# Decode attention with Mish: wq of the first pair whole ahead of the keys, b1 in one transfer, the residual in seven small transfers

## The chip, the core and the metric

The kernel runs on one core of one Trainium2 chip. TensorE (PE) multiplies, VectorE (DVE), ScalarE (ACT) and GpSimd (POOL) do the elementwise work, and SyncE (SP) issues most transfers between the chip's HBM and the on-chip memory SBUF. The transfers of all issuers are carried by the core's 16 DMA engines. The metric is the time of one execution on the device in microseconds. Everything is float32.

## The reference

Eight decode tokens, each with its own cache of 8192 keys and values for 8 key/value heads; four query heads share one of these. Beside the attention runs a dense block with Mish, and both are added to the input.

```python
xn = _layernorm(x, axis=-1)                                     # x: 8 x 1 x 512
q = (xn @ wq).reshape(B, 1, 32, 128)                            # wq: 512 x 4096
scores = einsum("bhqd,bhkd->bhqk", q, k) * (128 ** -0.5)        # k, v: 8 x 8 x 8192 x 128
o = einsum("bhqk,bhkd->bhqd", _softmax(scores), v)
A = o.reshape(B, 1, 4096) @ wo
h = xn @ w1 + b1                                                # w1: 512 x 1792
act = h * tanh(softplus(h))
return x + A + act @ w2
```

## The kernel before

**Units.** The key/value heads are taken in four pairs, and a unit is one pair of heads of one token: 32 units, numbered j, eight tokens b for each pair m. A unit's keys are 128 partitions of 64 KB (8.39 MB), its values are as large. The main loop (L483) runs over the units and does, for unit j: the scores in two halves (L316), a softmax (L328 to L349), the values of unit j - 1 (L378), the key weights of unit j + 1 (L299), the turning of the probabilities into the form that the value product needs (L355 to L366), and the merge of unit j - 1 (L395). The program's order is written out by hand; nothing is rescheduled. Each engine runs its own instructions in that order and waits only for what it needs.

**Places in SBUF.** One large tile `kv` holds what streams in. Values of all units, and the keys of unit 0, go to V_AT = 0. Keys of later units go alternately to two places (`K_AT`) that overlap by half: 16384 (even units) and 24576 (odd units), each 16384 elements wide. At 16384 also lie, at the start, the rows of x and the LayerNorm's scratch, then w1 (7168 elements) with b1 behind it, and then Mish's scratch. A second tile, `ws`, holds wq's columns of one pair (2 MB when whole).

**The loads on SP's queue.** SP issues, in order: three quarters of wq for pair 0 (L153), the keys of unit 0 (K0, through `load_unit`, L131), w1 (L476), the keys of unit 1 (K1), the values of unit 0 (V0), K2, V1, K3 and so on; wq for the later pairs (L125) comes in between, and wo and w2 at the end. An issue waits on SP until its place is free: V0 waits for the scores of unit 0, which read K0 at the same place; K2 waits until Mish has done with its scratch and until the first half of unit 1's scores has been read; V1 waits for the value product of unit 0.

**The last quarter of wq.** For pair 0 the projection `project(0)` (L245) takes its last 128 rows of wq from another place: `q0_x`, 32 partitions of `kv` at column 24576 (`XAT`), the place of the odd units' keys. Four transfers from POOL's queue (L150) fill it, alternating with four for b1 (L147), each of 8 partitions. Those issues stand on POOL ahead of the identity matrix (L158), the constants and the memsets, from which VectorE makes its selection matrices before it starts the LayerNorm (L188 to L201). Because three quarters of wq lie on 128 partitions and one quarter on 32, the transposed input exists in two extra forms, `xn3` (L208, L220) and `xnx` (L212, L221), beside `xn4`, which the later pairs use, and `xnT`, which Mish uses. A half of `project(0)` is three products on `ws` and four on `q0_x` (L255), then a copy by ACT (L263) and four small products (L266). `spread` (L281, L288) and `key_weights` (L299) follow before the scores of unit 0 can start.

**The residual.** x, as the last addition (L550) wants it, 8 rows at each of partitions 0, 32, 64 and 96, is made at the start by four products from `x_sb` with a copy into `xres` (L224 to L232).

Of the kernel before, what the change touches and what calls it, by code (L numbers as in the profile page):

```python
# [8 lines left out]
F32 = mybir.dt.float32  # L9
# [4 lines left out]
P = 128  # L14
B = 8
# [9 lines left out]
G = 4  # L25
NH = 2
TG = SK // (NH * G) // P
BW = 1024
CC = D // P
FG = F // G  # L30
FT = 4
FP = FG // FT
Q = P // G
# [4 lines left out]
ROW = NB * P * BW // P  # L38
# [13 lines left out]

D3 = 3
XQ = slice(64, 96)
XAT = ROW + ROW // 2

V_AT = 0
K_AT = (ROW, ROW + ROW // 2)
W1_AT = ROW
# [2 lines left out]


LOAD_Q, MAKE_Q, SPREAD_Q = 4, 5, 7


@with_exitstack
def kernel(
# [12 lines left out]
    nc = tc.nc  # L85
    PSUM = bass.MemoryType.PSUM

    const = ctx.enter_context(tc.tile_pool(name="const", bufs=1))
# [4 lines left out]
    kv = const.tile([P, PLACES], F32, name="kv")  # L93
    ws = const.tile([P, CC * BW], F32, name="ws")
# [4 lines left out]
    M = psum.tile([P, 512], F32, name="m")  # L99
    H = psum.tile([P, 512], F32, name="h")  # L100

    ident = const.tile([P, P], F32, name="ident")
# [7 lines left out]
    gsel = const.tile([B, B, B], F32, name="gsel")  # L110
    xn4 = const.tile([P, CC, B], F32, name="xn4")
    xnT = const.tile([P, CC, B], F32, name="xnT")
    xn3 = const.tile([P, D3, B], F32, name="xn3")
    xnx = const.tile([P, CC, B], F32, name="xnx")
    qr = const.tile([P, DI, H2 * B], F32, name="qr")
    xres = const.tile([P, P], F32, name="xres")
    oT = const.tile([P, NP, H2, B], F32, name="oT")
# [4 lines left out]
    def load_q(m):  # L122

        rows = wq.rearrange("j p f -> (j p f)").rearrange("(m p f) -> m p f", m=NP, p=P)
        nc.sync.dma_start(ws, rows[m])  # L125

    def load_unit(src, j, at):
        m, b = divmod(j, B)
        lo = (b * HKV + 2 * m) * NH * G
        t = kv[:, at : at + ROW]  # L130
        nc.sync.dma_start(  # L131
            t,
            src[lo : lo + NB].rearrange("j p f -> (j p f)").rearrange("(p f) -> p f", p=P),
        )
        return t
# [3 lines left out]
    x_sb, xc, sq = (low[:, i * D : (i + 1) * D] for i in range(3))  # L139
    nc.scalar.dma_start(x_sb, x)  # L140
    b1_sb = kv[:B, W1_AT + 7168 : W1_AT + 7168 + FG // 2]
    q0 = wq[:CC].rearrange("j p f -> (j p) f")
    q0_3 = ws[:, : D3 * BW]
    q0_x = kv[XQ, XAT : XAT + CC * BW]
    for r in range(4):
        n = FG // 8
        nc.gpsimd.dma_start(  # L147
            b1_sb[:, n * r : n * (r + 1)], b1.rearrange("(g c f) -> c g f", g=B, c=4)[r]
        )
        nc.gpsimd.dma_start(  # L150
            q0_x[r::4], q0[D3 * P :].rearrange("(e r i) f -> r e (i f)", r=4, i=CC)[r]
        )
    nc.sync.dma_start(q0_3, q0[: D3 * P].rearrange("(p i) f -> p (i f)", i=D3))  # L153
    k_t = {0: load_unit(kT, 0, V_AT)}
    w1_t = kv[:, W1_AT : W1_AT + 7168].rearrange("p (j f) -> p j f", j=2 * CC)

# [47 lines left out]
    for c in range(CC):  # L204
        nc.tensor.transpose(
            M[:, 32 + c * B : 32 + (c + 1) * B], xc[:, c * P : (c + 1) * P], ident[:B, :B]
        )
    for c in range(D3):  # L208
        nc.tensor.transpose(
            M[:, 64 + c * B : 64 + (c + 1) * B], xc[:, c : D3 * P : D3], ident[:B, :B]  # L210
        )
    for c in range(CC):  # L212
        nc.tensor.matmul(
            M[XQ, 96 + c * B : 96 + (c + 1) * B],
            xc[:, D3 * P + c :: CC],
            ident[:B, :B],
            start=True,
            stop=True,
        )
    nc.vector.tensor_copy(xn3.rearrange("p c b -> p (c b)"), M[:, 64 : 64 + D3 * B])  # L220
    nc.vector.tensor_copy(xnx[XQ].rearrange("p c b -> p (c b)"), M[XQ, 96:128])  # L221
    nc.vector.tensor_copy(xn4.rearrange("p c b -> p (c b)"), M[:, 0:32])
    nc.vector.tensor_copy(xnT.rearrange("p c b -> p (c b)"), M[:, 32:64])
    for g in range(G):  # L224
        nc.tensor.matmul(
            M[Q * g : Q * g + B, 256:384],
            ident[:B, :B],
            x_sb[:, g * P : (g + 1) * P],
            start=True,
            stop=True,  # L230
        )
    nc.vector.tensor_copy(xres, M[:, 256:384])  # L232
    wide = tr.rearrange("p y c -> p (y c)").rearrange("p (i o) -> p i o", i=DI)

    def selections():
# [9 lines left out]
    def project(m):  # L245

        w = ws.rearrange("p (c f) -> p c f", c=CC)
        terms = [(c, xn4[:, c, :], w[:, c]) for c in range(CC)]
        if m == 0:
            wx = q0_x.rearrange("p (c f) -> p c f", c=CC)  # L250
            terms = [(c, xn3[:, c, :], w[:, c]) for c in range(D3)]
            terms += [((c + D3) % CC, xnx[XQ, c, :], wx[:, c]) for c in range(CC)]
        for d in range(2):
            for n, (c, xt, wt) in enumerate(terms):
                nc.tensor.matmul(  # L255
                    H[Q * c : Q * c + B, :],
                    xt,
                    wt[:, d * 512 : (d + 1) * 512],
                    start=(n < CC),
                    stop=(n >= len(terms) - CC),  # L260
                )
            qp = work.tile([P, 512], F32, name="e")
            nc.scalar.copy(qp, H)  # L263
            for h in range(REP):
                at = 192 + (d * REP + h) * B
                nc.tensor.matmul(  # L266
                    M[:, at : at + B],
                    qp[:, h * DH : (h + 1) * DH],
                    bsel[:, :B],
                    start=True,  # L270
                    stop=True,
                )
        qT = work.tile([P, H2 * B], F32, name="qT", bufs=1)
        nc.vector.tensor_scalar_mul(qT, M[:, 192 : 192 + H2 * B], DH**-0.5)
        return qT
# [18 lines left out]
    def key_weights(j):  # L294
        b = j % B
        w = WK[j] = work.tile([P, DI, 2, NH * G, REP], F32, name="wk", bufs=1)
        q = qr.rearrange("p i (d o h b) -> p i d o h b", d=2, o=1, b=B)[..., b]
        for d in range(2):
            nc.vector.tensor_mul(  # L299
                w[:, :, d],  # L300
                q[:, :, d].to_broadcast([P, DI, NH * G, REP]),
                mask[:, d * NH * G : (d + 1) * NH * G]
                .rearrange("p (o k r) -> p o k r", o=1, r=1)
                .to_broadcast([P, DI, NH * G, REP]),
            )


    def scores(j, k, first, part):

        w = WK[j]  # L310
        lo = 0 if first else DI // 2
        kk = k.rearrange("p (i c f) -> p i c f", i=DI, c=HALF)
        for n in range(DI // 2):
            i = lo + n
            for c in range(HALF):
                nc.tensor.matmul(  # L316
                    S[64 * c : 64 * (c + 1), :],
                    w[:, i].rearrange("p d k h -> p (d k h)"),
                    kk[:, i, c, :],
                    start=(part == 0 and n == 0),  # L320
                    stop=(part == 1 and n == DI // 2 - 1),
                )
# [51 lines left out]
    def values(j, vt):  # L374
        for n in range(NJ):
            l, c = divmod(n, HALF)
            q = n % G
            nc.tensor.matmul(  # L378
                O[Q * q : Q * (q + 1), :],
                pt8[:, c, TL * l : TL * (l + 1), :].rearrange("p t h -> p (t h)"),  # L380
                vt[:, 512 * n : 512 * (n + 1)],
                start=(n < G),
                stop=(n >= NJ - G),
            )
        os = work.tile([P, DH], F32, name="os", bufs=1)
        nc.vector.tensor_scalar(os, O[:, :DH], isel[:, 0:1], None, op0=ALU.mult)  # L386
        for i in range(1, TL):
            nc.vector.scalar_tensor_tensor(  # L388
                os, O[:, DH * i : DH * (i + 1)], isel[:, i : i + 1], os, op0=ALU.mult, op1=ALU.add
            )  # L390
        return os
# [87 lines left out]
    spread(qT)  # L479
    key_weights(0)  # L480

    v_t = {}
    for j in range(UNITS):  # L483
        b = j % B
        more = j // B + 1 < NP

        k = k_t.pop(j)
        scores(j, k, j % 2 == 1, 0)
        if j == UNITS - 1:
            v_t[j] = load_unit(v, j, K_AT[0])  # L490
        elif j > 0:
            k_t[j + 1] = load_unit(kT, j + 1, K_AT[(j + 1) % 2])
        scores(j, k, j % 2 == 0, 1)
        WK.pop(j)
        lsel = softmax(j)
        os = None
        if j > 0:
            os = values(j - 1, v_t.pop(j - 1))
        if j + 1 < UNITS:
            v_t[j] = load_unit(v, j, V_AT)  # L500
            if more and b == SPREAD_Q:
                spread(qT)
            key_weights(j + 1)
        if j == 0:
            mish(w1_t, b1_sb, kv[:, W1_AT : W1_AT + 6 * FG])
        if more and b == LOAD_Q:
            load_q(j // B + 1)
        if more and b == MAKE_Q:
            qT = project(j // B + 1)
        turn(j, lsel)  # L510
        if j > 0:
            merge(j - 1, os)
        if more and b == SPREAD_Q - 1:
            selections()
# [24 lines left out]
    for g in range(G):  # L539
# [4 lines left out]
            start=False,  # L544
            stop=False,
# [44 lines left out]
```

## Time and profile before

| | us |
|---|---|
| time, median of 3 runs | 1331.87 |
| lowest and highest run | 1331.69, 1333.33 |
| span of the profiled execution | 1330.5 |
| PE busy | 984.8 |
| DVE busy | 516.0 |
| ACT busy | 40.2 |
| POOL busy | 6.4 |

The profile is of one execution; its span runs from its first to its last instruction. Busy times of the engines overlap. A row of the timeline gives the start, the duration, the engine with the source line, the operation, output <- input, and how often; what stands in brackets is the idle time before it and what ended it. SPq, ACTq and similar are an engine's sequencer, issuing a transfer. The share of the DMA engines in a window can exceed 1, since a packet is booked where it ends. In the list of transfers the last number is the median time from issue to landing. TensorE runs a float32 product in two passes, so the counts of the profile (x8) are twice the products of the program (x4).

### The profile page before, as it was taken

To read this page: it belongs to the slowest core of one execution; us is meant where nothing else is said; L and a number is where in the kernel's file an instruction comes from. 1 tells how busy PE (TensorE), PEld (TensorE's weight loads), DVE (VectorE), ACT (ScalarE), POOL (GpSimd) and SP (SyncE) were. 2 spreads that over 40 slices of the span, in tenths; PEclk is the share of its full clock that TensorE was granted. 3 is DMA by queue.
4 is the path that set the end of the run, shared out by engine and by line. 5 is a ranking of instruction groups with operands and counts; after the bars stand their busy time and mean duration, and the time that the engine had idled before them with its cause. 6 is when DMAs were issued, how large, how long until landed. Compare 5 with 4: busy or idle time off the path is not lost.

```text
span 1330.5 us, 11234 instructions
## 1 busy us (share of the span) xinstructions
PE 984.8 (74%) x5071; PEld 338.3 (25%) x5071; DVE 516.0 (39%) x730; ACT 40.2 (3%) x88; POOL 6.4 (0%) x17
## 2 busy tenths in 40 slices
PE   1888776877867976776887777687786787677766
PEld 0422222222322222222322222222232222222222
DVE  2065444134443234444244444413444332444431
ACT  1000000000000000000000000000000000000000
POOL 1000000000000000000000000000000000000000
PEclk9999789988889888879988888998897998888898
DMA  9889999999999999999999999999999999999997
GB/s 341 338 346 432 420 438 436 436 428 436 428 436 434 434 432 428 427 439 438 426 432 432 438 430 434 426 438 434 430 430 434 432 434 436 428 428 434 430 415 321
DMA packets 13839, 561.79 MB, mean 422 GB/s; under 512 B 1464, under 2 KB 1592, under 8 KB 4800
## 3 DMA queue, kind: packets, MB, share of 16 engines
q1 hardware_dynamic: 13520, 560.53, 98.2%
q8 instruction: 39, 0.64, 0.2%
q0 software_dynamic: 256, 0.53, 0.1%
q10 hardware_dynamic: 16, 0.02, 0.0%
q14 instruction: 8, 0.07, 0.0%
HBM read 561.01 MB, written 0.07 MB: 422 GB/s over the span
## 4 chain that ended last, share of the span: by engine, by line
DMA 73%; PE 22%; DVE 2%; SPq 2%; issue 0%; POOL 0%; ACT 0%; DVEq 0%; POOLq 0%
DMA kv<-in_v 70%; PE o L378 19%; DMA kv<-in_wq 2%; DMA kv<-in_w 2%; SPq L528 2%; PE s L316 1%; DVE pt L366 1%; PE x L281 1%; PE h L255 0%; PE m L266 0%; PE h L403 0%; DVE kv L434 0%; DVE tr L360 0%; POOL kv L147 0%; DVE wk L299 0%
## 5 line engine op out<-in xcount | busy, mean ns | idle before, releaser
L316 PE MATMUL s<-kv,wk 128*64 128x512 f32 x2048 | 505.7, 657 | 180.7 <-DMA kv<-in_kT 178.1
L378 PE MATMUL o<-kv,pt 128*32 128x512 f32 x2048 | 262.3, 671 | 51.8 <-DMA kv<-in_v 42.2
L316 PEld LDWEIGHTS s<-kv,wk 128*64 128x64 f32 x2048 | 156.0, 152 | 505.0 <-issue 321.5
L366 DVE TENSOR_REDUCE pt<-tr 64x512 f32<-64x2048 f32 x64 | 241.3, 3771 | 1.6
L328 DVE TENSOR_REDUCE nm<-s 128x1 f32<-128x512 f32 x32 | 22.1, 692 | 374.2 <-PE s L316 374.1
L355 PE MATMUL x<-e,perm 128*128 128x512 f32 x256 | 126.4, 639 | 2.0 <-ACT qr L288 2.0
L378 PEld LDWEIGHTS o<-kv,pt 128*32 128x32 f32 x2048 | 68.4, 122 | 219.3 <-issue 164.9
L386 DVE TENSOR_SCALAR os<-o,isel 128x128 f32<-128x128 f32 x32 | 11.2, 351 | 265.4 <-PE o L378 265.4
L360 DVE STREAM_TRANSPOSE tr<-x 128x512 f32<-128x512 f32 x128 | 78.6, 671 | 0.0
L299 DVE TENSOR_TENSOR wk<-qr,mask 128x512 f32<-128x512 f32 x64 | 63.0, 1026 | 19.8 <-ACT qr L288 19.8
L355 PEld LDWEIGHTS x<-e,perm 128*128 128x128 f32 x256 | 48.9, 201 | 74.6 <-issue 72.2
L347 ACT ACTIVATE e<-s,nmx 128x512 f32<-128x512 f32 x32 | 22.0, 688 | 1092.8 <-DVE nmx L344 1092.8
L388 DVE SCALAR_TENSOR_TENSOR os<-o,isel,os 128x128 f32<-128x128 f32 x96 | 33.7, 351 | 3.4
L329 PE MATMUL m<-ident,nm 128*1 128x128 f32 x32 | 8.7, 273 | 30.1 <-DVE nm L328 30.1
L340 PE MATMUL m<-ident,nx 1*128 1x1 f32 x32 | 7.0, 219 | 24.2 <-DVE nx L336 24.2
L281 PE MATMUL x<-qT,tr 128*128 128x64 f32 x128 | 19.3, 315 | 3.0 <-ACT qr L288 2.7
L358 DVE RECIPROCAL rt<-m 128x8 f32<-128x8 f32 x32 | 6.6, 208 | 34.0 <-PE m L356 34.0
L281 PEld LDWEIGHTS x<-qT,tr 128*128 128x128 f32 x128 | 18.1, 226 | 6.2 <-ACT qr L288 3.3
L395 PE MATMUL m<-hsel,os 128*128 128x8 f32 x64 | 12.4, 266 | 9.3 <-DVE rt L358 9.3
L349 DVE TENSOR_SCALAR lsel<-rsel,l 128x8 f32<-128x8 f32 x32 | 7.4, 231 | 30.1 <-ACT e L347 30.1
L329 PEld LDWEIGHTS m<-ident,nm 128*1 128x1 f32 x32 | 2.5, 79 | 58.3 <-DVE nm L328 58.3
L356 PEld LDWEIGHTS m<-lsel,ones 128*128 128x128 f32 x64 | 12.2, 190 | 15.6 <-issue 15.3
(98 smaller groups left out, 172.2 us busy)
## 6 DMA issues: line engine op xcount, KB each, us to landing
kv<-in_wo SPq DMA_DIRECT2D x4, 2048.0 KB, 25.9
ws<-in_wq SPq DMA_DIRECT2D x3, 2048.0 KB, 35.2
kv<-in_w SPq DMA_DIRECT2D x1, 3584.0 KB, 24.7
kv<-in_w SPq DMA_DIRECT2D x1, 2048.0 KB, 37.0
ws<-in_wq SPq DMA_DIRECT2D x1, 1536.0 KB, 7.6
kv<-in_w SPq DMA_DIRECT2D x1, 1024.0 KB, 20.7
kv<-in_kT SPq DMA_DIRECT2D x32, 29.5
kv<-in_wq POOLq DMA_DIRECT2D x4, 128.0 KB, 25.1
```

Of the source, the lines that this page charges most:

```text
L281: nc.tensor.matmul(X[:, half, k * 64 : (k + 1) * 64], wide[:, half * 8 + k], qT, start=True, stop=True,)
L299: nc.vector.tensor_mul(w[:, :, d], q[:, :, d].to_broadcast([P, DI, NH * G, REP]), mask[:, d * NH * G : (d + 1) * NH * G] .rearrange("p (o ...
L316: nc.tensor.matmul(S[64 * c : 64 * (c + 1), :], w[:, i].rearrange("p d k h -> p (d k h)"), kk[:, i, c, :], start=(part == 0 and n == 0), s ...
L328: nc.vector.tensor_reduce(nm, S, axis=AX.X, op=ALU.max, negate=True)
L347: nc.scalar.activation(e, S, AF.Exp, bias=nmx, accum_out=l)
L355: nc.tensor.matmul(X[:, g], perm[:, g], e, start=True, stop=True)
L360: nc.vector.transpose(tr.rearrange("p (l t) c -> p t l c", t=TL)[:, tl], X.rearrange("p g (t q l) -> p t l g q", t=TL, q=PP)[:, tl],)
L366: nc.vector.tensor_reduce(pt8[half, :, :, d * REP : (d + 1) * REP].rearrange("p c y h -> p y c h"), tr[half].rearrange("p y (g c h) -> p y ...
L378: nc.tensor.matmul(O[Q * q : Q * (q + 1), :], pt8[:, c, TL * l : TL * (l + 1), :].rearrange("p t h -> p (t h)"), vt[:, 512 * n : 512 * (n ...
L388: nc.vector.scalar_tensor_tensor(os, O[:, DH * i : DH * (i + 1)], isel[:, i : i + 1], os, op0=ALU.mult, op1=ALU.add)
L395: nc.tensor.matmul(M[:, 168 : 168 + H2], os, hsel, start=True, stop=True)
L528: nc.sync.dma_start(t, w2_rows[:, lo * BW : hi * BW])
```

## The change

`project(0)` now takes wq whole from `ws`, like the later pairs. SP's first transfer is `load_q(0)`, 128 rows of 16 KB, ahead of K0. `q0_x`, `xn3`, `xnx`, their seven transposes and two copies are gone, and so are POOL's eight transfers. b1 comes by one transfer of 8 rows of 896 B on ACT's queue, behind x. The four products that made `xres` and their copy are gone: `xres` is set to zero by POOL, and seven transfers from x on ACT's queue fill its 32 rows, one in each of units 9 to 15, of 1, 7, 2, 6, 3, 5 and 8 rows of 512 B.

```diff
+CUTS = ((0, 0, 1), (0, 1, B), (1, 0, 2), (1, 2, B), (2, 0, 3), (2, 3, B), (3, 0, B))
...
-    q0 = wq[:CC].rearrange("j p f -> (j p) f")
-    q0_3 = ws[:, : D3 * BW]
-    q0_x = kv[XQ, XAT : XAT + CC * BW]
-    for r in range(4):
-        n = FG // 8
-        nc.gpsimd.dma_start(
-            b1_sb[:, n * r : n * (r + 1)], b1.rearrange("(g c f) -> c g f", g=B, c=4)[r]
-        )
-        nc.gpsimd.dma_start(
-            q0_x[r::4], q0[D3 * P :].rearrange("(e r i) f -> r e (i f)", r=4, i=CC)[r]
-        )
-    nc.sync.dma_start(q0_3, q0[: D3 * P].rearrange("(p i) f -> p (i f)", i=D3))
+    nc.scalar.dma_start(b1_sb, b1.rearrange("(g f) -> g f", g=B))
+    load_q(0)
     k_t = {0: load_unit(kT, 0, V_AT)}
...
-    for g in range(G):
-        nc.tensor.matmul(
-            M[Q * g : Q * g + B, 256:384],
-            ident[:B, :B],
-            x_sb[:, g * P : (g + 1) * P],
-            start=True,
-            stop=True,
-        )
-    nc.vector.tensor_copy(xres, M[:, 256:384])
...
-        if m == 0:
-            wx = q0_x.rearrange("p (c f) -> p c f", c=CC)
-            terms = [(c, xn3[:, c, :], w[:, c]) for c in range(D3)]
-            terms += [((c + D3) % CC, xnx[XQ, c, :], wx[:, c]) for c in range(CC)]
...
+    def residual(g, lo, hi):
+
+        nc.scalar.dma_start(
+            xres[Q * g + lo : Q * g + hi, :], x[lo:hi, g * P : (g + 1) * P]
+        )
+
+    nc.gpsimd.memset(xres, 0.0)
...
+        if 9 <= j < 9 + len(CUTS):
+            residual(*CUTS[j - 9])
```

How the instructions stand on three engines, before and after. First SP, from the program's start: the loads in order, each with the shape of what it writes and the semaphores that it waits for (DMASW are completions of POOL's transfers, DMAHW those of SP's and ACT's, the others name engines). Before:

```order
L153 DMA ws<-in_wq 128x3072
L131 DMA kv<-in_kT 128x16384
L476 DMA kv<-in_w 128x8x896 [waits DVE_49,DMAHW0_49,PE_49,Activation_49]
L131 DMA kv<-in_kT 128x16384 [waits DMASW5_49,DMASW3_49,DMASW7_49,DMASW1_49,PE_49]
L131 DMA kv<-in_v 128x16384 [waits DMAHW2_49,PE_49]
```

After:

```order
L119 DMA ws<-in_wq 128x4096
L125 DMA kv<-in_kT 128x16384
L433 DMA kv<-in_w 128x8x896 [waits DVE_49,DMAHW0_49,PE_49,Activation_49]
L125 DMA kv<-in_kT 128x16384
L125 DMA kv<-in_v 128x16384 [waits DMAHW3_49,PE_49]
```

The order of the loads is the same. The second keys (K1) waited for four of POOL's transfers and for PE, and now wait for nothing.

Next POOL, from the end of its start-up to the memset of the probabilities' tile `pt`, before:

```order
L147 DMA kv<-in_b 8x56
L150 DMA kv<-in_wq 8x4096
L147 DMA kv<-in_b 8x56
L150 DMA kv<-in_wq 8x4096
L147 DMA kv<-in_b 8x56
L150 DMA kv<-in_wq 8x4096
L147 DMA kv<-in_b 8x56
L150 DMA kv<-in_wq 8x4096
masks.py:197 MEMSET ident 128x128
```

After:

```order
masks.py:197 MEMSET ident 128x128
masks.py:199 ISA
masks.py:199 AFFINE_SELECT ident<-ident 128x128 [waits Pool_49]
L143 MEMSET ones 128x128
L144 MEMSET perm 128x512
L145 MEMSET pt_88 128x1024
L445 MEMSET xres 128x128
```

The eight issues ahead of the identity matrix are gone, and a memset of `xres` stands last.

Last PE, from its first product to the spread of the queries (h is the projection's sum, m a scratch tile, xn_84 and xn_82 are `xn3` and `xn4`). Before:

```order
L203 MATMUL m<-ident,kv 128x8 x4
L205 MATMUL m<-ident,kv 128x8 x4
L209 MATMUL m<-ident,kv 128x8 x3
L213 MATMUL m<-ident,kv 32x8 x4
L225 MATMUL m<-kv,ident 8x128 x4
L255 MATMUL h<-ws,xn_84 8x512 x3
L255 MATMUL h<-kv,xnx 8x512 x4
L266 MATMUL m<-bsel,e 128x8 x4
L255 MATMUL h<-ws,xn_84 8x512 x3
L255 MATMUL h<-kv,xnx 8x512 x4
L266 MATMUL m<-bsel,e 128x8 x4
```

After:

```order
L187 MATMUL m<-ident,kv 128x8 x4
L189 MATMUL m<-ident,kv 128x8 x4
L212 MATMUL h<-ws,xn_82 8x512 x4
L223 MATMUL m<-bsel,e 128x8 x4
L212 MATMUL h<-ws,xn_82 8x512 x4
L223 MATMUL m<-bsel,e 128x8 x4
L238 MATMUL x_69<-qT,tr 128x64 x16
```

Eleven small products (L209 to L225) are gone, and each half of the projection has four products in place of seven, all on `ws`.

More of the change, by code (lines that the diff above doesn't have):

```diff
@@ L51 @@
 W2R = 7
-D3 = 3
-XQ = slice(64, 96)
-XAT = ROW + ROW // 2
 V_AT = 0
@@ L112 @@
     xnT = const.tile([P, CC, B], F32, name="xnT")
-    xn3 = const.tile([P, D3, B], F32, name="xn3")
-    xnx = const.tile([P, CC, B], F32, name="xnx")
     qr = const.tile([P, DI, H2 * B], F32, name="qr")
@@ L207 @@
         )
-    for c in range(D3):
-        nc.tensor.transpose(
-            M[:, 64 + c * B : 64 + (c + 1) * B], xc[:, c : D3 * P : D3], ident[:B, :B]
-        )
-    for c in range(CC):
-        nc.tensor.matmul(
-            M[XQ, 96 + c * B : 96 + (c + 1) * B],
-            xc[:, D3 * P + c :: CC],
-            ident[:B, :B],
-            start=True,
-            stop=True,
-        )
-    nc.vector.tensor_copy(xn3.rearrange("p c b -> p (c b)"), M[:, 64 : 64 + D3 * B])
-    nc.vector.tensor_copy(xnx[XQ].rearrange("p c b -> p (c b)"), M[XQ, 96:128])
     nc.vector.tensor_copy(xn4.rearrange("p c b -> p (c b)"), M[:, 0:32])
     nc.vector.tensor_copy(xnT.rearrange("p c b -> p (c b)"), M[:, 32:64])
-    for g in range(G):
-        nc.tensor.matmul(
-            M[Q * g : Q * g + B, 256:384],
-            ident[:B, :B],
-            x_sb[:, g * P : (g + 1) * P],
-            start=True,
-            stop=True,
-        )
-    nc.vector.tensor_copy(xres, M[:, 256:384])
     wide = tr.rearrange("p y c -> p (y c)").rearrange("p (i o) -> p i o", i=DI)
```

## The prediction

> **What bounds the kernel now.** I read the page's slices and queue table first, then its chain.
>
> ```profile
> span 1330.5 us, 11234 instructions
> DMA  9889999999999999999999999999999999999997
> GB/s 341 338 346 432 420 438 436 436 428 436 428 436 434 434 432 428 427 439 438 426 432 432 438 430 434 426 438 434 430 430 434 432 434 436 428 428 434 430 415 321
> q1 hardware_dynamic: 13520, 560.53, 98.2%
> DMA 73%; PE 22%; DVE 2%; SPq 2%; issue 0%; POOL 0%; ACT 0%; DVEq 0%; POOLq 0%
> ```
>
> The DMA engines are busy in every slice, and SP's queue alone fills 98.2% of their time. No engine comes near that. So the end is set by when those 560.53 MB have been moved, and time is lost only where the stream stands still or slows. The first three slices move 338 to 346 GB/s, the middle ones about 432. That is where I look next, by the table of windows (duration, busy us and count of PE, PEld, DVE, ACT and POOL, the granted clock, DMA share, GB/s).
>
> ```profile
> core 0: us, PE busy (x) PEld busy (x) DVE busy (x) ACT busy (x) POOL busy (x), PEclk, DMA share, GB/s
> 0.00:27.00 27.00, 4.37 (x33) 2.09 (x33) 9.13 (x34) 3.49 (x5) 6.45 (x17) 1.00 0.99 372
> 27.00:34.00 7.00, 0.00 (x0) 0.00 (x0) 0.00 (x0) 0.00 (x0) 0.00 (x0) 1.00 0.78 220
> 34.00:39.00 5.00, 4.25 (x19) 2.04 (x22) 0.00 (x0) 0.59 (x1) 0.00 (x0) 1.00 1.03 406
> 39.00:42.00 3.00, 3.00 (x14) 0.12 (x8) 0.00 (x0) 0.00 (x0) 0.00 (x0) 1.00 0.47 188
> 42.00:62.00 20.00, 15.65 (x60) 10.62 (x58) 2.17 (x3) 1.76 (x3) 0.00 (x0) 1.00 0.99 417
> 62.00:73.00 11.00, 10.56 (x50) 3.23 (x46) 0.39 (x1) 0.00 (x0) 0.00 (x0) 1.00 0.02 6
> 73.00:93.00 20.00, 18.89 (x110) 6.83 (x112) 16.07 (x30) 2.64 (x4) 0.00 (x0) 1.00 1.01 420
> 93.00:120.00 27.00, 20.55 (x114) 6.83 (x112) 17.43 (x22) 0.78 (x2) 0.00 (x0) 0.87 0.99 426
> 120.00:160.00 40.00, 28.94 (x138) 9.11 (x136) 20.91 (x24) 0.78 (x2) 0.00 (x0) 0.84 1.02 441
> 160.00:1280.00 1120.00, 846.91 (x4240) 286.68 (x4240) 436.30 (x601) 29.61 (x70) 0.00 (x0) 0.88 1.00 432
> ```
>
> From 62 to 73 us nothing moves (6 GB/s). From 27 to 34 and from 39 to 42 the rate is about half. From 73 us on there is no further hole: the share is 0.97 to 1.02 all the way. Which issue ends each hole is in the timeline of SP's queue.
>
> ```profile
> 0.74 0.38 SPq L153 DMA_DIRECT2D ws<-in_wq  x1
> 1.19 0.42 SPq L131 DMA_DIRECT2D kv<-in_kT  x1
> 17.63 0.38 SPq L476 DMA_DIRECT2D kv<-in_w  x1
> 42.20 0.34 SPq L131 DMA_DIRECT2D kv<-in_kT  x1
> 72.60 0.33 SPq L131 DMA_DIRECT2D kv<-in_v  x1
> 90.79 0.33 SPq L131 DMA_DIRECT2D kv<-in_kT  x1
> 111.55 0.33 SPq L131 DMA_DIRECT2D kv<-in_v  x1
> ```
>
> In order: wq, K0, w1, K1, V0, K2, V1. V0 goes out at 72.60, because it overwrites K0 and so waits for the last score product of unit 0. K1 goes out at 42.20, because it overwrites the last quarter of wq and waits for the projection. The chain says why both are late.
>
> ```profile
> 4.97 28.93 DMA kv<-in_wq
> 34.05 1.92 PE h L255 x8
> 38.50 3.68 PE h L255 x14
> 55.72 16.86 PE s L316 x64
> ```
>
> The last quarter of wq, loaded by POOL, lands at 33.9 us, 28.93 us after its issue began. The projection's remaining products then run at 34.05, and the scores from 55.72 to 72.58.
>
> **The change, part by part.**
>
> *K1.* Its place is no longer used for wq, and the order lists no wait for it. It follows w1 on SP at once, at the latest at 18 us instead of 42.20. All that V0 follows is then queued by then: wq 2.10, K0 8.39, w1 3.67, K1 8.39, together 22.55 MB. Before, the same 22.55 MB (73 us at a mean of 309 GB/s) took until V0's data began at 73.
>
> *Stream to the end of K1.* In the first 27 us 27 x 0.372 = 10.04 MB moved; at the 417 GB/s of 42 to 62 that is 24.1 us, so the stream effectively starts at 2.9. After the change K1 ends at 2.9 + 22.55/0.417 = 57.0 us. At the steady 432 GB/s it would be 3.8 + 52.2 = 56.0. V0's data could begin there instead of at 73: **16.0 to 17.0 us** earlier, if V0 has been issued by then.
>
> *Is V0 issued in time?* The beginning of the program, in rows of the timeline:
>
> ```profile
> 1.26 0.65 POOL L147 DMA_DIRECT2D kv<-in_b  x1 [0.82 <-POOLq L577]
> 5.49 0.22 POOL masks.py:197 MEMSET ident<- 128x128 f32 x1
> 6.72 0.99 DVE L169 COPY perm<-ident 128x16 f32<-128x16 f32 x8 [4.23 <-POOL perm L160]
> 9.01 0.67 DVE L188 TENSOR_REDUCE st<-kv 8x1 f32<-8x512 f32 x1
> 13.57 0.47 DVE L201 TENSOR_SCALAR kv<-kv,st 8x512 f32<-8x512 f32 x1
> 14.66 0.57 PE L205 MATMUL m<-ident,kv 8*128 8x8 f32 x4
> ```
>
> POOL's eight issues took 1.26 to 5.49, 4.23 us, and VectorE idled those same 4.23 us behind POOL. They go, so L188 can start at 4.78 if x has landed, and at 9.01 at the latest seen so far. From L188 to the end of the L205 transposes is 15.23 - 9.01 = 6.22; with an estimated 0.3 for the copy that follows it is 6.5, since the transposes of L209, L213 and L225 are gone. So the projection can start at 11.3 to 15.5. Is wq there?
>
> ```profile
> ws<-in_wq SPq DMA_DIRECT2D x1, 1536.0 KB, 7.6
> ...
> kv<-in_wq POOLq DMA_DIRECT2D x4, 128.0 KB, 25.1
> ...
> kv<-in_b POOLq DMA_DIRECT2D x4, 1.8 KB, 21.2
> out<-os SPq DMA_DIRECT2D x1, 64.0 KB, 1.5
> ```
>
> The 1.57 MB of wq took 7.6 us; 0.52 MB more at 417 GB/s is 1.3, so it lands at 0.74 + 8.9 = 9.6, before the projection wants it. From the projection's restart (34.05) to V0's issue (72.60) is 38.55; the second half's 14 passes (3.68) become 8 (1.92), which leaves 36.8. V0's issue comes at **48.1 to 52.3 us**, against 56.0 to 57.0 for the end of K1: 4 to 9 us of cover. K0 has to be there too. Its landing, from the issue at 1.19:
>
> ```profile
> DMA to landing us min/median/max: 31.2/31.2/31.2
> ```
>
> That is 32.4 us with the slow stretch inside it; the scores start at 31.2 to 35.4, so even an unchanged K0 moves V0 to 49.3 at most in the early case.
>
> *What is late next?* K2 waits for Mish, 90.79 - 72.60 = 18.2 us behind V0's issue, so at 66 to 71; V0 itself streams from 56 to 76. V1 waits for the first value product, 38.95 behind, at 87 to 91; K2 streams until 95. So the next waits are covered by 4 to 5 us or more, and the lead passes through to a steady stream, which ends everything. From 73 to 120 us the old kernel moved 423 GB/s on average with one transfer queued at times; with two queued, 432 gives 47 x (1 - 423/432) = 1.0 us more. Bound from below: 0.
>
> *b1 in one transfer from ACT.* One more issue on ACT, as long as x's:
>
> ```profile
> 0.74 0.59 ACTq L140 DMA_DIRECT2D kv<-in_x  x1
> ```
>
> Those 0.59 us stand ahead of ACT's first square, which the LayerNorm wants only after 5. Its four predecessors took 21.2 us to land beside K0; even so it is there at 25, and Mish reads it after 50. Cost 0.
>
> *The residual.* Four products and a copy at the start go. A memset on the idle POOL and seven issues on ACT come, in units 9 to 15. Between its exponentials ACT is idle:
>
> ```profile
> L347 ACT ACTIVATE e<-s,nmx 128x512 f32<-128x512 f32 x32 | 22.0, 688 | 1092.8 <-DVE nmx L344 1092.8
> ```
>
> 1092.8 us over 32 is 34 us each, so 0.59 us of issue hides. They are read only by the last addition. What they take from the stream no row shows: 32 rows of 512 B are 16 KB, 0.04 us at 432 GB/s; from above, 1.5 us each, as the output takes from issue to landing, is 10.5 us. I take 0, since b1's four, of like size, lie in a window (0 to 27 us) that still moved 372 GB/s with its start in it. The Trainium skill ("DMA: Bandwidth & Descriptors", Rules for kernel authors) speaks against this part: coalesce many small transfers, under 64 KB mostly overhead is paid; its section on the anatomy of a DMA puts the fixed cost at about 2.0 us. Were all of that taken out of the stream, it would be an estimated 14 us; the same section calls it mostly completion latency, and the trace's 1.5 us cannot tell the two apart.
>
> *Sum.* 16.0 to 17.0 plus 0 to 1.0, less 0: a gain of 16 to 18, I take **17.2**. The profiled span of 1330.5 becomes 1313.3; the median of the runs is 1331.87, 1.4 above that span, so 1314.7.
>
> **Rivals.**
>
> 1. *The slow stretch stays.* If 27 to 42 us is slow because of w1's own short pieces, w1 still ends at 42, K1 follows until 62, and the gain is 73 - 62 = 11: 1321. For it: half the rate begins when w1 begins. Against: w1 alone moves 406 GB/s from 34 to 39, directly after POOL's pieces have landed at 33.9.
> 2. *Small transfers stop the stream* for as long as one takes to land: 7 x 1.5 = 10.5 back, 1325. It is what the page's rule amounts to, which with its own figure gives an estimated 1329.
> 3. *Small transfers stop it for longer: slower.* Place: units 9 to 15. One turn of the stream, 64 KB on each of 16 engines, is 1.05 MB/417 = 2.5 us. If each of the seven held all engines for one turn, 17.6 us would cancel the gain; from there on it is slower: two turns give 1350. Against: eight small transfers from POOL in the first 27 us would have cost 20 us by that price, and 372 GB/s leave room for some 3.
> 4. *x comes late: nothing gained.* V0's issue is L188 + 43.3 us. If x had to queue behind K0 as b1 did, L188 at 29 would put V0 at 72.6 again and the time at 1332: the change moves bytes and does not do what it says. Against: before, x was there by 9.01, issued beside the same kind of load; only 4 KB a row are added in front.
>
> **How the numbers follow.** Forecast (1312 to 1317) 0.78; slow stretch stays 0.10; rival 2 0.05; rival 4 0.04; rival 3 0.03. The range 1311 to 1321.5 takes in the forecast, the upper rates and rival 1. A difference of 0.2% (2.7 us) is about what a measurement of this kernel tells from none. Faster: 0.78 + 0.10 + 0.05 = 0.93; same 0.04; slower 0.03.
>
> **What would show it.** In the profile after: wq by one landing near 9.6; projection at 11 to 16; K1 issued right behind w1; no idle window before 73; V0 issued at 48 to 52, its data beginning near 56; the first three slices near 400 GB/s, the later ones at 432 as before; in units 9 to 15 no dip. Wrong would be: a first L188 after 14, which uses up V0's cover; a rate below 400 between 27 and 42; an idle stretch ahead of K2 or V1; or a dip in the slices around 400 to 660 us, where units 9 to 15 run.

## The result, and the profile after

| | before | after |
|---|---|---|
| median of the runs, us | 1332.60 | 1313.06 |
| lowest and highest, us | 1331.69, 1333.87 | 1312.63, 1313.82 |
| span of the profiled execution, us | 1330.5 | 1310.8 |

The changed kernel takes 0.9858 of the time before (95% interval 0.9844 to 0.9871): 19.5 us less in the medians, 19.7 in the spans. The forecast was 17.2 less. Two of all the executions timed here ran at a lower granted clock (0.65) and took 1413.5 and 1437.2 us; no median below counts them.

The page of the changed kernel, its slices, queue and chain:

```profile
span 1310.8 us, 11161 instructions
DMA  9999999999999999999999999999999999999998
GB/s 393 450 422 439 426 438 428 431 440 426 438 424 440 431 434 425 445 420 443 423 438 433 429 436 424 440 428 436 426 437 430 434 432 436 428 436 428 433 411 324
q1 hardware_dynamic: 13520, 561.06, 99.3%
DMA 72%; PE 23%; DVE 2%; SPq 1%; issue 0%; ACT 0%; DVEq 0%
```

SP's queue now fills 99.3% of the DMA engines' time in place of 98.2%. The first three slices, at 338 to 346 GB/s before, now move 393 to 450; the rest is as it was. Nearly all of the difference lies in the first 100 us. The windows of the changed kernel, with the columns and bounds of those shown of before:

```profile
0.00:27.00 27.00, 14.76 (x68) 10.84 (x69) 8.30 (x32) 5.25 (x8) 2.35 (x10) 1.00 0.93 390
27.00:34.00 7.00, 4.36 (x14) 1.92 (x15) 1.93 (x2) 0.59 (x1) 0.00 (x0) 1.00 1.01 408
34.00:39.00 5.00, 5.00 (x22) 1.53 (x20) 0.00 (x0) 0.00 (x0) 0.00 (x0) 1.00 1.36 569
39.00:42.00 3.00, 3.00 (x18) 0.98 (x15) 0.00 (x0) 0.00 (x0) 0.00 (x0) 1.00 0.81 350
42.00:62.00 20.00, 18.07 (x108) 6.68 (x106) 10.84 (x20) 2.64 (x4) 0.00 (x0) 1.00 0.98 423
62.00:73.00 11.00, 9.44 (x45) 3.46 (x40) 10.75 (x13) 0.00 (x0) 0.00 (x0) 1.00 1.07 460
73.00:93.00 20.00, 13.07 (x78) 4.46 (x78) 10.71 (x20) 0.78 (x2) 0.00 (x0) 0.83 0.98 423
```

The row that read 6 GB/s (62 to 73 us) reads 460, and the one that read 220 (27 to 34) reads 408. A window of a few microseconds can show 569 or 350, since a packet is booked whole in one window: in that in which it starts, and not, as was said ahead of the prediction, where it ends. The kernel before shows this right behind V0's issue at 72.60:

```profile
72.00:73.00 1.00, 0.56 (x4) 0.00 (x0) 0.39 (x1) 0.00 (x0) 0.00 (x0) 1.00 0.00 0
73.00:74.00 1.00, 0.27 (x1) 0.08 (x1) 0.64 (x3) 0.00 (x0) 0.00 (x0) 1.00 2.96 983
75.00:76.00 1.00, 1.00 (x16) 0.24 (x12) 0.00 (x0) 1.00 (x1) 0.00 (x0) 1.00 0.00 0
```

Into one microsecond fall 983 GB/s, 15 packets of 64 KB, with 2.96 us of work for each DMA engine in the mean. Had they ended there, they would have begun before V0 was issued. So where a row first reads 0, the engines still work on the last packets, for up to 2.4 us; the times of the packets themselves are in the trace, and I use them below.

Summed over these packets, a DMA engine was idle for 19.8 us in the mean before and for 6.0 after, and busy for 1310.9 and 1305.0. So of the 19.7 us, 13.8 are idle time that is gone, and 5.9 are packets that take less time: one of 64 KB that starts before 25 us took 2.75 us in the mean before, beside POOL's transfers, and takes 2.42 now.

SP's queue in the same execution:

```profile
0.74 0.36 SPq L119 DMA_DIRECT2D ws<-in_wq  x1
1.15 0.42 SPq L125 DMA_DIRECT2D kv<-in_kT  x1
10.68 0.38 SPq L433 DMA_DIRECT2D kv<-in_w  x1
11.11 8.94 SPq L125 DMA_DIRECT2D kv<-in_kT  x1
47.36 0.33 SPq L125 DMA_DIRECT2D kv<-in_v  x1
65.58 0.33 SPq L125 DMA_DIRECT2D kv<-in_kT  x1
86.19 0.33 SPq L125 DMA_DIRECT2D kv<-in_v  x1
```

K1 goes out at 11.11 us in place of 42.20, and V0 at 47.36 in place of 72.60. The steps that lead to V0, in the timeline: LayerNorm's first reduction, the projection, the scores of unit 0.

```profile
4.38 0.67 DVE L172 TENSOR_REDUCE st<-kv 8x1 f32<-8x512 f32 x1
10.88 1.90 PE L212 MATMUL h<-ws,xn 128*8 128x512 f32 x8 [0.28 <-DVE xn L192]
30.75 16.56 PE L273 MATMUL s<-kv,wk 128*64 128x512 f32 x64 [2.64 <-DVE wk L256]
```

The projection waits for VectorE's copy only; wq is there. It starts 23.17 us earlier than the restart at 34.05.

### The profile page after: what moved, and what is told of

The parts are those of the page before. It is cut to its first block, busy times and chain, and to the rows that moved or that the text cites. A ratio compares the mean times of both kernels' runs of the same rounds, so it can differ in the third digit from the quotient of the medians.

```text
span 1310.8 us, 11161 instructions
## 1 busy us (share of the span) xinstructions
PE 996.7 (76%) x5040; PEld 342.2 (26%) x5040; DVE 514.9 (39%) x727; ACT 40.2 (3%) x88; POOL 2.4 (0%) x10
## 3 DMA queue, kind: packets, MB, share of 16 engines
q1 hardware_dynamic: 13520, 561.06, 99.3%
## 4 chain that ended last, share of the span: by engine, by line
DMA 72%; PE 23%; DVE 2%; SPq 1%; issue 0%; ACT 0%; DVEq 0%
DMA kv<-in_v 70%; PE o L335 20%; DMA kv<-in_w 2%; SPq L494 1%; PE s L273 1%; DVE pt L323 1%; PE x L238 1%; PE h L212 0%; PE m L223 0%; PE h L360 0%; DVE kv L391 0%; DVE tr L317 0%; DVE wk L256 0%; DVE nm L285 0%; ACT L179 0%
## 5 line engine op out<-in xcount | busy, mean ns | idle before, releaser
L335 PE MATMUL o<-kv,pt 128*32 128x512 f32 x2048 | 273.7, 695 | 51.0 <-DMA kv<-in_v 41.4
L312 PE MATMUL x<-e,perm 128*128 128x512 f32 x256 | 129.2, 651 | 2.0 <-ACT qr L245 2.0
L256 DVE TENSOR_TENSOR wk<-qr,mask 128x512 f32<-128x512 f32 x64 | 63.0, 1025 | 19.8 <-ACT qr L245 19.8
L238 PEld LDWEIGHTS x<-qT,tr 128*128 128x128 f32 x128 | 18.1, 226 | 6.2 <-ACT qr L245 3.3
## 6 DMA issues: line engine op xcount, KB each, us to landing
kv<-in_wo SPq DMA_DIRECT2D x4, 2048.0 KB, 22.9
```

What stands on the lines that cost most here:

```text
L238: nc.tensor.matmul(X[:, half, k * 64 : (k + 1) * 64], wide[:, half * 8 + k], qT, start=True, stop=True,)
L256: nc.vector.tensor_mul(w[:, :, d], q[:, :, d].to_broadcast([P, DI, NH * G, REP]), mask[:, d * NH * G : (d + 1) * NH * G] .rearrange("p (o ...
L312: nc.tensor.matmul(X[:, g], perm[:, g], e, start=True, stop=True)
L335: nc.tensor.matmul(O[Q * q : Q * (q + 1), :], pt8[:, c, TL * l : TL * (l + 1), :].rearrange("p t h -> p (t h)"), vt[:, 512 * n : 512 * (n ...
```

## The experiments

Every kernel was timed beside the kernel before. Times are medians.

### The changed kernel again

No edit; the base for the others.

> The changed kernel again, as the base of the runs beside it: 1313 us, a ratio of 0.986 to the kernel before. V0 issued at 47.4 us, no idle window before 73 us.

1313.42 us (ratio 0.9856, 0.9841 to 0.9871), V0 issued at 46.25 us. The base for what follows is taken as 1313.4.

### The projection made late by 2 us

```diff
+    for _ in range(2):
+        nc.vector.memset(tr, 0.0)
     nc.vector.tensor_copy(xn4.rearrange("p c b -> p (c b)"), M[:, 0:32])
```

> The changed kernel with two memsets of a 128 x 2048 tile (about 1.9 us each) on VectorE ahead of the copy that the projection waits for, so that V0's issue moves from 47.4 to about 51.2 us. Theory (the end is set by when the transfers have run, and V0 only has to be issued before K1 has streamed, at about 54.5 us): hidden, 1313 us within 1. Rival (the gain is the earlier projection itself, passed on one for one): 1317 us.

1312.88 us. V0 went out at 49.22 us, 3.0 later than in the run above, and the time did not move: hidden, as the theory said. The memsets moved it by less than the 3.8 us expected against the 47.4 of the changed kernel, so this is a test of 2 to 3 us only.

### The projection made late by 18 us

The same loop with nine memsets.

> The same with nine memsets, about 17.2 us: V0's issue at about 64.6 us, 10 us after K1 has streamed at about 54.5. Theory: an idle stretch of about 10 us opens and the time is 1321 to 1324 us. Rival one for one: 1330 us. Rival that the freed issue of K1 alone makes the gain: 1313 us.

1326.92 us (ratio 0.9958, 0.9944 to 0.9972), 13.5 us more than the base. V0's issue and two windows of this kernel:

```profile
65.37 0.33 SPq L125 DMA_DIRECT2D kv<-in_v  x1
...
0.00:54.00 54.00, 20.33 (x84) 13.14 (x86) 25.92 (x43) 5.83 (x9) 2.46 (x10) 1.00 0.99 418
54.00:66.00 12.00, 11.32 (x54) 3.51 (x50) 0.62 (x1) 0.00 (x0) 0.00 (x0) 1.00 0.01 1
```

V0 goes out 18.0 us later than in the changed kernel, and 13.5 of these are lost: neither one for one nor nothing. In the first 54 us 54 x 0.418 = 22.57 MB are begun, which is just wq, K0, w1 and K1; then no packet starts until V0's. K1's last packets end at 55.4 us in the mean, and V0's first starts at 66.34, 1.0 us after its issue. So the hole is 10.9 us, close to the 10 expected, and the point from which a late V0 costs is 65.4 - 10.9 = 54.5 us, as expected.

The time still lies 3 us above the expected 1321 to 1324. Two things had been left out. V1, issued at 105.48, came too late as well: K2's last packets end at 106.1 in the mean and V1's first starts at 106.45, which costs another 0.9 us of idle engines. And the first packet on each engine after the hole takes 3.0 us in place of 2.4. What remains, about 1 us, stays open; the runs of this kernel spread from 1325.76 to 1328.35.

### K1 held until the key weights are written

```diff
-    k_t[1] = load_unit(kT, 1, K_AT[1])
     spread(qT)
     key_weights(0)
+    nc.vector.tensor_copy(kv[:, K_AT[1] : K_AT[1] + 1], WK[0][:, 0, 0, 0, 0:1])
+    k_t[1] = load_unit(kT, 1, K_AT[1])
```

> The changed kernel with K1's issue held until the key weights of unit 0 are written (by a one-element copy by VectorE into K1's place): issued at about 31 us instead of 11. Theory: w1 streams until about 35 us, so K1 is still queued in time: 1313 us within 1. Rival (K1 must be free at once, and the deeper queue makes the higher rate): the first windows fall back to 417 GB/s and the time is 1315 us or more.

1313.51 us with K1 issued at 30.74. The theory held: with the projection early, 20 us of delay for K1 cost nothing, since w1 still streams then. K1's first packet starts at 35.7 us in this run and in the changed kernel alike.

### Only wq's part of the change

```diff
-    nc.scalar.dma_start(b1_sb, b1.rearrange("(g f) -> g f", g=B))
+    for r in range(4):
+        n = FG // 8
+        nc.gpsimd.dma_start(
+            b1_sb[:, n * r : n * (r + 1)], b1.rearrange("(g c f) -> c g f", g=B, c=4)[r]
+        )
...
+    for g in range(G):
+        nc.tensor.matmul(M[Q * g : Q * g + B, 256:384], ident[:B, :B], x_sb[:, g * P : (g + 1) * P], start=True, stop=True)
+    nc.vector.tensor_copy(xres, M[:, 256:384])
...
-    nc.gpsimd.memset(xres, 0.0)
...
-        if 9 <= j < 9 + len(CUTS):
-            residual(*CUTS[j - 9])
```

> wq whole by one transfer ahead of K0, but b1 by four transfers of POOL and the residual by four products and a copy at the start, as in the kernel before; no small transfers in units 9 to 15. Theory: POOL's four issues (2.1 us) and the products put V0's issue at about 50.5 us, still before 54.5: 1313 us within 1, so all of the gain is wq's. Rival 2 of the prediction (each small transfer costs 1.5 us): this one is 10 us faster than the changed kernel, 1303 us.

1312.82 us (ratio 0.9856, 0.984 to 0.9871). V0 goes out at 50.95, still hidden. Given wq whole on SP's queue, the other two edits change nothing that these runs can tell, and the seven small transfers cost nothing.

### Only the other two parts of the change

```diff
+    nc.scalar.dma_start(b1_sb, b1.rearrange("(g f) -> g f", g=B))
     q0 = wq[:CC].rearrange("j p f -> (j p) f")
     for r in range(4):
-        n = FG // 8
-        nc.gpsimd.dma_start(
-            b1_sb[:, n * r : n * (r + 1)], b1.rearrange("(g c f) -> c g f", g=B, c=4)[r]
-        )
...
         if 9 <= j < 9 + len(CUTS):
+            residual(*CUTS[j - 9])
```

The edits stand on the kernel before; the products for `xres` go, as in the change.

> The kernel before with only the other two edits: b1 by one transfer on ACT's queue and the residual by seven small transfers, with the last quarter of wq still by POOL into K1's place. Theory (the gain is all wq's): the quarter's issues end 2 us earlier, its landing beside the keys does not move by more than that: 1330 to 1333 us. Rival (b1's four transfers on POOL's queue delayed the quarter): the quarter lands near 22 us, as the one transfer of POOL did, and the time is 1322 us or less.

1324.81 us (ratio 0.9943, 0.9925 to 0.996): 8.7 us less than the 1333.55 beside it. Both missed, the theory by 5 us and the rival by 3; the rival came closer, though its landing at 22 us is one at 24.96. Six runs spread from 1322.67 to 1331.38, so its size is known to a few microseconds. The chain, V0's issue and POOL's queue (packets, MB, share of the span) of this kernel:

```profile
2.91 22.05 DMA kv<-in_wq
...
63.33 0.33 SPq L133 DMA_DIRECT2D kv<-in_v  x1
...
q0 software_dynamic: 128, 0.52, 0.1%
```

And POOL's queue in the kernel before:

```profile
q0 software_dynamic: 256, 0.53, 0.1%
```

Without b1, which is 7 KB in all, POOL's queue has half the packets, and the quarter of wq lands at 24.96 us in place of 33.90. Of these 8.94 us, 2.06 are its last issue, which comes earlier (2.91 in place of 4.97). In the kernel before, b1's 32 packets of 224 B start between 5.3 and 31.4 us, among the quarter's 32 of 16 KB (6.0 to 31.8; without b1, 5.6 to 20.9); the rest of the 256 are of 4 B. So b1 stood among the quarter, and not ahead of it.

The page "DMA: Bandwidth & Descriptors" of the Trainium skill (Queues, rings and completion order) says that a DMA engine takes turns between its queues packet by packet. The trace agrees: in the run with only wq's part, b1's transfers have POOL's queue to themselves, 128 packets of 0.01 to 0.02 us each, and these start from 5.6 to 17.6 us, beside keys whose 64 KB packets take 2.42 us. That each of b1's packets cost the quarter such a turn is how I read it; no row names a packet's engine, so that b1 also changed which engines carry the quarter is a rival left open.

### The quarter of wq by POOL, but in one transfer of 128 rows

```diff
-    load_q(0)
+    q0 = wq[:CC].rearrange("j p f -> (j p) f")
+    nc.gpsimd.dma_start(ws[:, 3 * BW :], q0[3 * P :])
+    nc.sync.dma_start(ws[:, : 3 * BW], q0[: 3 * P].rearrange("(p i) f -> p (i f)", i=3))
...
+        if m == 0:
+            terms = [(c, xn3[:, c, :], w[:, c]) for c in range(3)]
+            terms += [(3, xnT[:, 3, :], w[:, 3])]
```

> The changed kernel with the last quarter of wq taken from POOL again, but as one transfer onto 128 partitions x 4 KB into the free quarter of ws, so that K1's place stays free and the projection waits for it. Theory (that queue gets its turn between packets of the other, so 8 small packets for each DMA engine come through while wq and the first keys stream): it lands well before 20 us and V0 is issued in time: 1313 to 1315 us. Rival (a transfer from POOL beside the keys lands at 25 us or later, as before): the projection starts there, V0's issue comes at 62 us or later, 1320 us or more.

1320.58 us (ratio 0.9913, 0.9897 to 0.9928). The theory fell on the landing. The chain and V0's issue of this kernel:

```profile
1.23 21.66 DMA ws<-in_wq
...
59.25 0.33 SPq L126 DMA_DIRECT2D kv<-in_v  x1
```

It lands at 22.9 us, not well before 20, though sooner than the rival's 25, and V0 follows at 59.25, sooner than the rival's 62. The time is up by 7.2 us. K1's last packets end at 55.4 us in the mean and V0's first starts at 60.2: a hole of 4.8. V1, issued at 99.66 with K2's packets ending at 100.0, opens one of 1.1, and V0's first packets take 3.1 us in place of 2.4. So it is the same account as with nine memsets, with 0.6 us open.

### Transfers from POOL that nobody reads

The changed kernel, with 0.52 MB from POOL added at K1's place: four transfers of 8 partitions x 16 KB, or one of 128 partitions x 4 KB.

```diff
+    q1 = wq[CC : 2 * CC].rearrange("j p f -> (j p) f")
+    spare = kv[64:96, K_AT[1] : K_AT[1] + CC * BW]
+    for r in range(4):
+        nc.gpsimd.dma_start(spare[r::4], q1[3 * P :].rearrange("(e r i) f -> r e (i f)", r=4, i=CC)[r])
```

```diff
+    spare = kv[:, K_AT[1] : K_AT[1] + BW]
+    nc.gpsimd.dma_start(spare, q1[3 * P :])
```

> The changed kernel with POOL's four transfers of 8 partitions x 16 KB put back, of rows of wq that nobody reads, at their old place (so K1 waits for their landing, but the projection does not). Theory (these transfers made the slow stretch of 27 to 42 us): the rate falls to about 220 GB/s from 27 us until they land at about 34, and w1 ends near 41; of the cover some is used, and the time is 1316 to 1319 us. Rival (0.52 MB more to move and nothing else): 1314.3 us.

> The changed kernel with the same 0.52 MB by one transfer from POOL onto 128 partitions x 4 KB, at K1's place, read by nobody. Theory (it is the 8 partitions of each transfer that make some DMA engines late, not POOL's queue): no slow stretch, 0.52 MB at 432 GB/s is 1.2 us: 1314.3 us within 1. Rival (any transfer from POOL beside the keys slows the stream): as with 8 partitions, 1316 to 1319 us.

Four transfers of 8 partitions: 1318.56 us, 5.1 more. One of 128 partitions: 1314.64, 1.2 more, which is what its bytes take at 432 GB/s. Both hold the expected times. The first windows, of the first kernel and then of the second:

```profile
0.00:27.00 27.00, 12.19 (x56) 8.27 (x56) 8.71 (x32) 5.25 (x8) 4.67 (x14) 1.00 0.97 350
27.00:34.00 7.00, 3.84 (x18) 3.68 (x20) 1.94 (x2) 0.59 (x1) 0.00 (x0) 1.00 0.86 360
```

```profile
0.00:27.00 27.00, 13.73 (x63) 9.81 (x64) 8.71 (x32) 5.25 (x8) 3.15 (x11) 1.00 0.98 409
27.00:34.00 7.00, 4.37 (x17) 2.72 (x18) 1.92 (x2) 0.59 (x1) 0.00 (x0) 1.00 0.84 336
```

V0 went out at 50.81 and 48.70 us, both hidden, so the difference lies in the stream: 27 x (0.409 - 0.350) = 1.6 MB less by 27 us, 3.7 us at 432 GB/s, and the two times differ by 3.9. The loss shows in the first window and not, as I had expected, as 220 GB/s from 27 to 34. The packets tell where it goes: those of 64 KB that start before 25 us take 2.75 us in the mean beside the four transfers and 2.42 beside the one, while the DMA engines are idle for only 0.1 us longer in the first 120 us. So the stream's own packets are slowed. That these four transfers do it is shown; whether by their 8 partitions, by their number or by their packets of 16 KB (4 KB in the one transfer) is not, since all three differ.

### More small transfers

Each of the seven issued five times in a row to the same rows; one in each of units 1 to 28; each issued four times to four different sets of rows.

```diff
-            residual(*CUTS[j - 9])
+            for _ in range(5):
+                residual(*CUTS[j - 9])
```

```diff
-        if 9 <= j < 9 + len(CUTS):
-            residual(*CUTS[j - 9])
+        if 1 <= j < 29:
+            residual(*CUTS[(j - 1) % 7])
```

```diff
-            residual(*CUTS[j - 9])
+            g, lo, hi = CUTS[j - 9]
+            for n in range(4):
+                nc.scalar.dma_start(xres[Q * g + B * n + lo : Q * g + B * n + hi, :], x[lo:hi, g * P : (g + 1) * P])
```

> The changed kernel with each of the seven small transfers issued five times in a row, 35 in place of 7. Theory (each costs the stream about nothing): 1313 us within 1. Rival 2 of the prediction (1.5 us each): 28 more cost 42 us, 1355 us. In between, the difference over 28 is the price of one.

> The changed kernel with one small transfer in each of the units 1 to 28, the seven row cuts four times over, 28 in place of 7. Theory: 1313 us within 1. Rival 2: 21 more at 1.5 us, 1344.5 us. If the cost is one per unit that holds a transfer rather than one per transfer, this one is dearer than the one with five in a row.

> The changed kernel with each of the seven small transfers issued four times, to four different sets of rows of xres (the three further sets are rows that are not part of the result): 28 in place of 7, in bursts of four. The run with five in a row to the same rows took 1318 us, and in its trace ACT stands before one exponential and one copy until a small transfer has landed. Theory (that cost is the order of writes to the same rows, which makes ACT wait for each landing, and not the transfers' own use of the stream): without it 1313 us within 1. Rival (a burst of small transfers takes time from the stream, 0.17 us each as in that run): 21 more cost 3.6 us, 1317 us.

1318.23, 1313.51 and 1313.84 us. Spread over the units or in bursts, 21 more transfers cost 0.1 to 0.8 us together, by which of the two medians of the changed kernel is the base (1313.42 or 1313.06): within what the runs can tell. The burst of five cost 4.8 us (runs from 1316.19 to 1321.59), and its chain around 548 us says why:

```profile
547.62 3.74 DMA xres<-in_x
...
551.38 8.54 DMA xres<-in_x
...
559.94 8.18 DMA xres<-in_x
...
568.14 7.27 DMA xres<-in_x
...
575.78 0.59 ACT e L220
```

Each transfer waits on ACT until the one before it, which writes the same rows, has landed; one takes 4 to 9 us beside the stream, and the projection's copy stands behind them on ACT until 575.78. The scores of the next unit, and with them the issue of the keys that follow, come late: SP's issue at 583.16 in the changed kernel comes at 596.97, and the stream has a hole of 8.2 us in this execution, the slowest of its four. The first line is of this run, the second of the run with different rows:

```profile
580.00:600.00 20.00, 18.94 (x72) 8.41 (x70) 10.52 (x9) 0.59 (x1) 0.00 (x0) 0.79 0.59 240
580.00:600.00 20.00, 17.89 (x102) 5.18 (x102) 1.71 (x7) 0.78 (x2) 0.00 (x0) 0.91 0.99 429
```

The other six bursts open none. With different rows the four issues of a burst go out back to back, here the exponential of unit 10 and its transfers:

```profile
431.83 0.69 ACT L304 ACTIVATE e<-s,nmx 128x512 f32<-128x512 f32 x1 [39.05 <-DVE nmx L301]
431.88 0.62 ACTq L471 DMA_DIRECT2D xres<-in_x  x2
...
432.55 0.94 ACTq L471 DMA_DIRECT2D xres<-in_x  x2
```

So a small transfer costs the stream nothing that can be seen, and its landing costs whoever waits for it.

## Why the prediction was right, point by point

*The bound.* Right. The end follows the stream. In the kernels with a hole ahead of V0, the span less V0's issue is nearly one number: before 1330.5 - 72.60 = 1257.9, with nine memsets 1326.6 - 65.37 = 1261.2, with the two other edits 1320.9 - 63.33 = 1257.6, with the quarter in one transfer 1319.1 - 59.25 = 1259.9 us. The two larger ones are those in which V1 was late too.

*The sum.* The mechanism was right and two terms a little small. "Stream to the end of K1", 16.0 to 17.0 us, measured 18.1: V0's first packet started at 73.6 us before, where the sum has 73, and K1's last packets now end at 55.5 in the mean (55.1 to 56.9), with V0's right behind, where it has 56.0 to 57.0. The stream's start and rate came from windows that held what the change removes: the first 27 us, with POOL's transfers, moved 372 GB/s and move 390 without them, and the 417 of 42 to 62 hold the wait for K1's first packet, which starts at 43.2. Reading the windows as booked at the end works the other way and hid a part of this: the 10.53 MB of the first 27 us now would let K1 end at 27 - 24.4 + 52.2 = 54.8 at 432 GB/s, and it ended at 55.5. The term for the steady stream behind, 0 to 1.0, measured 1.6: the lead is 18.9 us where V0's packets end (93.9 before, 75.0 after, in the mean) and 19.7 at the end of the program. Most of the first 0.8 of that is V0's first packet on each engine, which took 3.1 us out of the standstill and now takes 2.4.

*V0's issue.* Forecast 48.1 to 52.3, measured 47.36, just below the early end: x had landed by 4.38 us. The cover, forecast as 4 to 9 us, is 54.5 - 47.4 = 7.1.

*K1 and what is late next.* Right: K2 at 65.58 and V1 at 86.19 come 18.2 and 38.8 us behind V0, as before, K2's issue 9 us ahead of the end of V0's packets and V1's 8 us ahead of the end of K2's, and no slice after shows a hole.

*b1 at a cost of 0.* Right as the change stands, by the run with wq alone. But the four transfers that went with it were costed as POOL's issue time only; in the old layout their going, with the products for `xres`, was worth 8.7 us without any change to wq, since the quarter was queued among them. The prediction had their row (21.2 us to land) and did not ask who was queued with them. That does not add to the sum: with wq whole on SP's queue nobody waits for POOL's.

*The residual.* Right: 0. *Rivals.* The slow stretch did not stay (408 GB/s from 27 to 34), so rival 1 is out; rivals 2 and 3 fall with the run without the seven transfers and the runs with more of them; rival 4 falls with L172 at 4.38. The Trainium skill's rule on small transfers, in "DMA: Bandwidth & Descriptors", does not hold as a cost of the stream here: 21 more took at most 0.8 us, where the 2.0 each that the prediction took from that page, which gives it for GpSimd's transfers, would be 42. As a cost of landing, 4 to 9 us beside a busy stream is more than that figure.

## What to carry to other kernels

Where one stream bounds a kernel, look for the issue that ends each hole and follow its wait back; moving it earlier pays until the transfer ahead has run out, and not beyond. A small transfer is cheap if nobody waits for it, but on a queue that shares DMA engines with long packets its packets can hold up what is queued among and behind them, as b1's did. An undisturbed rate must not be taken from a window that holds what the change removes, and the end of a stream not from a window that books packets where they start.

## What the runs showed of the hardware that was not expected

- 7 KB of b1 in four transfers from POOL went with 128 more packets on its queue (256 against 128), and half a megabyte queued among them landed 9 us later, 2 of these by its later issue.
- Four transfers onto 8 partitions each cost 3.9 us more than one onto 128 partitions with the same 0.52 MB; beside them the stream's 64 KB packets took 2.75 us in place of 2.42.
- From V0's issue to its first packet passed 0.95 to 0.97 us in the four kernels with a hole ahead of it, and the first packet on each engine then took 3.0 to 3.1 us in place of 2.4.
- K1's issue held SP for 8.94 us with wq, K0 and w1 queued ahead of it; issued at 30.74, in the run that held it, it took 0.34. Begun at 11.11, at 12.47 (quarter in one transfer) and at 14.71 (only wq's part), it ended at 20.05, 19.96 and 20.07, and begun at 21.68, beside the four transfers that nobody reads, at 25.78. So SP seems to wait for the stream to get to some point; for what, no row says. SP had nothing else to issue until V0, so it cost nothing.
